# Making the gate's constants in two steps instead of one

## The chip, the cores and the metric

The kernel runs on one core of a Trainium2 chip. The metric is the device time of one execution in microseconds (us), as the median of several. Five engines work side by side, each through its own list of instructions in a fixed order: TensorE (PE; its weight loads are shown as PEld), VectorE (DVE), ScalarE (ACT), GpSimd (POOL) and SyncE (SP), whose queue issues the loads. An instruction that waits holds up everything behind it on its engine.

## The reference, cut to what matters

An attention stage feeds a mixture of experts (four experts, each token gets a weighted sum of all), and that feeds a second mixture in which each token goes to one of eight experts. The change concerns the numbers that choose this expert:

```python
logits = x @ w_gate + modality_bias[modality_id]   # x: 1152 x 512, w_gate: 512 x 8
e_idx = np.argmax(logits, axis=1)
probs = softmax(logits)
gate_w = probs[np.arange(N), e_idx]
# for every expert e, on the tokens with e_idx == e:
out[mask] = gate_w[mask, None] * (np.maximum(x[mask] @ w1[e], 0.0) @ w2[e])
```

## The kernel before

**Tiling.** Tokens are worked on in four chunks of 256, 256, 256 and 384 (numbered 0 to 3), the 1024 hidden units of an expert in eight slices f = 0 to 7. float32 operands are split into a high and a low part, and a product is made of three matmuls (high by high, high by low, low by high). For one slice and chunk, `mm1` (L695, 12 matmuls) makes the hidden values in PSUM, ACT writes their high part `hh` (L701), DVE their low part `hl` (L706), and `mm2` (L719 to L721, 3 matmuls for each 128 tokens) multiplies them by the second weight matrix. The third matmul of `mm2` is the first that needs `hl`. The weights are split the same way, by ACT (L404) and DVE (L674).

**Segments.** The first mixture runs as nine segments (an expert and some chunks each). The place of interest is segment 4: expert 3 on chunk 2, then on chunk 3. The text below calls its steps (2, f) and (3, f) by chunk and slice, so mm1(2, 3) is `mm1` of chunk 2, slice 3. In program order a step is mm1 of this slice, then mm2 of the slice before, and between them some extra work. By then the rows of chunks 0 and 1 are final, so their part of the second gate can start: 32 dot products on DVE (`dot`, L982: one block of 128 tokens by one column of `w_gate`; in the trace each is one SCALAR_TENSOR_TENSOR and one DVE_READ_ACCUMULATOR), one `dot` call after each step.

**The gate's constants.** `gate_consts` (L900 on) is called at step (2, 1). It has GpSimd make small tables; stores a table of empty slots, `ti`, to memory (`tab`, L935); loads the gate's weights as `wr` (L937), which DVE splits into `wg` (L939, L940); loads the same weights four more times, spread over all partitions, as `st` (L945), which GpSimd copies into rows `wgT` (L946), which the dots read; loads the modality numbers `mi` (L948) and the bias rows `mb` (L950); has DVE turn `mi` into floats `mf` (L952), PE transpose them (L954), and DVE make `bias` of the result (L957 to L964). `gate_cols` at step (2, 4) lets GpSimd copy the last two columns into `wgU` (L970), and the dots start behind it.

**What sets the order.** `ti`, `wr`, `mi` and a scratch tile of the bias share one buffer, named "tmp", and so each of them waits until the one before has been used up. Outside the parts with an order written by hand, the framework's scheduler places the instructions of each engine from their order in the program and their dependences; an instruction can land some steps before or after the place where the code has it.

Of the kernel before, what the change touches and what calls it, by code (L numbers as in the profile page):

```python
# [8 lines left out]
F32 = mybir.dt.float32  # L9
F32R = mybir.dt.float32r  # L10
# [3 lines left out]
ALU = mybir.AluOpType  # L14
# [14 lines left out]
KD = DM // 128  # L29
# [15 lines left out]
FIRST = {0: 0, 1: 0, 2: 4, 3: 4}  # L45
# [244 lines left out]
def moe_chain_kernel(ctx, tc, q, k, v, probs, w1, w2, mod, wg, mbias, v1, v2, out):  # L290
    nc = tc.nc
    N, E = probs.shape
    NT = N // 128
# [587 lines left out]
    m2p = {}  # L881
    G = {}
    R = {}
    V = v1.shape[0]
# [21 lines left out]
    def gate_consts():  # L906
        g = m2p["g"]

        def t(name, shape, dt=F32):
            G[name] = g.tile(shape, dt, tag=name, name=name, bufs=1)  # L910
            return G[name]

        def io(name, shape, pattern, base=0, cm=0):
            a = t(name, shape)
            nc.gpsimd.iota(a, pattern=pattern, base=base, channel_multiplier=cm, allow_small_or_imprecise_dtypes=True)

        io("e8", [128, V], [[-1, V]], base=V)
        io("ei", [128, V], [[1, V]])
        io("en", [128, V], [[SLOTS, V]])
        io("j128", [128, NBLK], [[128, NBLK]])  # L920
        io("thr", [128, NT], [[128, NT]])
        io("thr64", [128, NT], [[128, NT]], base=64)
        io("j", [128, NBLK], [[1, NBLK]])
        up = g.tile([128, 128], F32, tag="upf", name="upf", bufs=1)
        nc.gpsimd.memset(up, 1.0)
        nc.gpsimd.affine_select(out=up, in_=up, pattern=[[1, 128]], compare_op=ALU.is_gt, fill=0.0,
                                base=0, channel_multiplier=-1)
        nc.gpsimd.tensor_copy(out=t("up", [128, 128], BF16), in_=up)
        nc.gpsimd.memset(t("one", [128, 128], BF16), 1.0)
        G["tg"] = t("tg", [128, NT, 2])  # L930
        nc.gpsimd.iota(G["tg"][:, :, 0:1], pattern=[[128, NT]], base=0, channel_multiplier=1, allow_small_or_imprecise_dtypes=True)
        ti = g.tile([128, 256], F32, tag="tmp", name="ti", bufs=1)[:, 0:CAP // 64].rearrange("p (n c) -> p n c", c=2)
        nc.gpsimd.memset(ti, 0.0)
        nc.gpsimd.memset(ti[:, :, 0:1], float(N))
        nc.sync.dma_start(out=tab.rearrange("(p n) c -> p n c", p=128), in_=ti)  # L935
        wr = g.tile([128, 256], F32, tag="tmp", name="wr", bufs=1)[:, 0:KD * V].rearrange("p (k e) -> p k e", k=KD)
        nc.sync.dma_start(out=wr, in_=wg.rearrange("(k p) e -> p k e", p=128))  # L937
        w = t("wg", [128, KD, 2 * V], F32R)
        nc.vector.tensor_copy(out=w[:, :, 0:V], in_=wr)  # L939
        nc.vector.tensor_tensor(out=w[:, :, V:2 * V], in0=wr, in1=w[:, :, 0:V].bitcast(F32), op=ALU.subtract)  # L940

        t("wgT", [128, V - 2, DM])
        for qq in range(KD):
            st = G["st", qq] = m2p["raw"].tile([128, 128, V], F32, tag=f"r{qq + 3}", name=f"st{qq}")
            nc.sync.dma_start(out=st.rearrange("p d e -> p (d e)"), in_=wg[128 * qq:128 * qq + 128].rearrange("d e -> (d e)").partition_broadcast(128))  # L945
            nc.gpsimd.tensor_copy(out=G["wgT"][:, :, 128 * qq:128 * qq + 128], in_=st[:, :, 0:V - 2].rearrange("p d e -> p e d"))  # L946
        mi = g.tile([128, 256], F32, tag="tmp", name="mi", bufs=1)[0:NT].bitcast(I32).rearrange("p (n c) -> p n c", c=2)
        nc.sync.dma_start(out=mi, in_=mod.bitcast(I32).rearrange("(i p two) -> i p two", p=128, two=2))  # L948
        mb = g.tile([128, 2, V], F32, tag="mb", name="mb", bufs=1)
        nc.sync.dma_start(out=mb, in_=mbias.rearrange("m e -> (m e)").partition_broadcast(128))  # L950
        mf = g.tile([NT, 128], F32, tag="mf", name="mf", bufs=1)
        nc.vector.tensor_copy(out=mf, in_=mi[:, :, 0])  # L952
        pt = bank()
        nc.tensor.transpose(pt[:, 0:NT], mf, ident[:NT, :NT])  # L954
        m = g.tile([128, NT, 1], F32, tag="m", name="m", bufs=1)
        m0 = g.tile([128, NT, 1], F32, tag="m0", name="m0", bufs=1)
        nc.vector.tensor_copy(out=m, in_=pt[:, 0:NT])  # L957
        nc.vector.tensor_scalar(out=m0, in0=m, scalar1=-1.0, scalar2=1.0, op0=ALU.mult, op1=ALU.add)
        b = t("bias", [128, NT, V])
        b1 = g.tile([128, 256], F32, tag="tmp", name="b1", bufs=1)[:, 0:NT * V].rearrange("p (n e) -> p n e", n=NT)  # L960
        sh = [128, NT, V]
        nc.vector.tensor_tensor(out=b, in0=m0.to_broadcast(sh), in1=bc(mb[:, 0, :], sh, 1), op=ALU.mult)
        nc.vector.tensor_tensor(out=b1, in0=m.to_broadcast(sh), in1=bc(mb[:, 1, :], sh, 1), op=ALU.mult)
        nc.vector.tensor_tensor(out=b, in0=b, in1=b1, op=ALU.add)  # L964
# [695 lines left out]
    if True:  # L1660
# [87 lines left out]
        dots = [(i, x) for i in range(4) for x in range(V)]  # L1748
        for s, c, f in late:
            mm1(s, c, f)  # L1750
            if prev[0] in PAIR:
                s_mm2(*units[-1])
                ctxs.close()
                m2p["raw"] = ctx.enter_context(tc.tile_pool(name="m2raw", bufs=1, side="right", reuse_waits="tile"))
                m2p["g"] = ctx.enter_context(tc.tile_pool(name="gate", bufs=2, side="right", reuse_waits="tile"))
                y1 = m2p["g"].tile([128, 5, DM], F32, tag="y1", name="y1", bufs=1)
                yacc.extend(y1[:, t, :] for t in range(5))
            else:
                mm2(*prev)
            prev = (s, c, f)  # L1760
            if (s, c) == late[0][:2] and f < 4:
                w_split(1 + f % 2, s, 2 + f // 2)
                if f < 2:
                    w_load(1 + f, s, 3)
            r = runs.index((s, c))
            if c == SEG[s][1][0] and s > late[0][0] and f < 2:
                w_split(1 + f, s, 3)
                if len(SEG[s][1]) == 1:
                    w_load(1 + f, s + 1, 0)
            if f >= 6 and s == runs[r + 1][0] and c == SEG[s][1][-2]:  # L1770
                w_load(f - 5, s + 1, 0)
            if c == SEG[s][1][-1] and f >= 2:
                j = f // 2 - 1
                kind = 1 + f % 2
                w_split(kind, s + 1, j)
                w_load(kind, s + 1, j + 1)
            if (s, c, f) == (FIRST[2], 2, 1):
                gate_consts()
            if (s, c, f) == (FIRST[2], 2, 4):
                gate_cols()  # L1780
            if (s, c, f) > (FIRST[2], 2, 4) and dots:
                dot(*dots.pop(0))

        Q = build2()
# [42 lines left out]
```

## Time and profile before

| | us |
|---|---|
| median of 3 runs | 631.9 |
| lowest, highest | 631.59, 633.16 |
| profiled execution | 637.08 |
| its span | 635.1 |
| busy: PE / DVE / ACT / POOL | 602.2 / 423.3 / 277.3 / 83.9 |
| granted TensorE clock, mean | 0.977 of full speed |

The page cuts the span into 40 slices of 15.9 us each. PE is 90% busy or more in most of them; the low one in the middle is the slice around 260 us, where PE shows 4 tenths and its clock 7 tenths. A mean over the span hides such a place, so it is read by windows and by the timeline of each engine. In a timeline a row gives the start, the duration, the instruction, and in brackets how long its engine sat idle before it and what ended that wait.

### The profile page before, as it was taken

What the parts mean: (1) busy time and instruction counts of PE and PEld (TensorE: products, weight loads), DVE (VectorE), ACT (ScalarE), POOL (GpSimd) and SP (SyncE); (2) the same over time, 40 slices, a digit from 0 to 9 for tenths busy, and PEclk for the clock granted to TensorE, in tenths of its full rate; (3) what the DMA queues carried; (4) which work ended last, traced back from release to release, by engine and by line L of the source; (5) the groups of instructions that cost most, each with busy time, mean ns of one, the idle gap of its engine ahead of it and who ended that gap; (6) DMA issues with size and microseconds to landing.
All of it is one profiled execution on the core that took longest, in us unless ns stands there. A gap on an engine that the chain in (4) does not pass through costs nothing.

```text
span 635.1 us, 11351 instructions
## 1 busy us (share of the span) xinstructions
PE 602.2 (95%) x4229; PEld 527.7 (83%) x4234; DVE 423.3 (67%) x883; ACT 277.3 (44%) x628; POOL 83.9 (13%) x120
## 2 busy tenths in 40 slices
PE   7889999999999999499999999999999987999994
PEld 4678888889998888399999989989988876898883
DVE  4988777769759956697342355449765768658781
ACT  4955256544435443013311334213243543559581
POOL 3342123100000001600000000020130142101011
PEclk8989999999999999799999999999999997999998
DMA  7999944103423345401330346505496221868930
GB/s 148 158 220 217 225 126 130 35 2 99 133 67 100 101 132 160 146 1 51 118 99 1 100 133 199 166 33 101 102 343 188 82 68 42 279 195 255 309 134 20
DMA packets 91890, 82.87 MB, mean 130 GB/s; under 512 B 36391, under 2 KB 73648, under 8 KB 91826
## 3 DMA queue, kind: packets, MB, share of 16 engines
q1 hardware_dynamic: 89906, 77.33, 43.7%
q0 software_dynamic: 1920, 4.73, 2.2%
q8 instruction: 35, 0.57, 0.4%
q14 instruction: 29, 0.24, 0.1%
HBM read 81.69 MB, written 5.07 MB: 137 GB/s over the span
## 4 chain that ended last, share of the span: by engine, by line
PE 85%; DVE 4%; issue 4%; DMA 2%; ACT 1%; POOL 1%; another core or an unknown queue 1%; SPq 1%; POOLq 0%; ACTq 0%
PE ps L695 27%; PE ps L719 11%; PE ps L721 10%; PE ps L720 10%; PE ps L1432 7%; PE ps L809 5%; PE ps L1455 2%; PE ps L1454 2%; PE ps L1456 2%; PE ps L585 1%; DMA kraw<-in_k_dram 1%; PE ps L400 1%; DMA st<-in_moe_w_gate_dram 1%; PE ps L456 1%
## 5 line engine op out<-in xcount | busy, mean ns | idle before, releaser
L695 PE MATMUL ps<-xhi,w1h 128*128 128x256 f32 (+1 forms) x416 | 128.0, 308 | 0.0
L695 PE MATMUL ps<-xlo,w1h 128*128 128x256 f32 (+1 forms) x416 | 125.7, 302 | 0.3 <-DVE xlo L599 0.3
L695 PE MATMUL ps<-xhi,w1l 128*128 128x256 f32 (+1 forms) x416 | 125.6, 302 | 0.0
L701 ACT ACTIVATE hh<-ps 128x256 fp32r<-128x256 f32 (+1 forms) x104 | 43.0, 414 | 165.1 <-PE ps L695 153.3
L719 PE MATMUL ps<-w2h,hh 128*128 128x512 f32 x240 | 96.6, 403 | 0.0
L706 DVE SCALAR_TENSOR_TENSOR hl<-ps,hh 128x256 fp32r<-128x256 f32 (+1 forms) x104 | 47.8, 461 | 72.0 <-ACT hh L701 71.6
L721 PE MATMUL ps<-w2h,hl 128*128 128x512 f32 x240 | 94.8, 395 | 0.7 <-DVE hl L706 0.7
L720 PE MATMUL ps<-w2l,hh 128*128 128x512 f32 x240 | 94.4, 393 | 0.0
L695 PEld LDWEIGHTS ps<-xhi,w1h 128*128 128x128 f32 x416 | 79.7, 191 | 4.8 <-issue 0.6
L695 PEld LDWEIGHTS ps<-xlo,w1h 128*128 128x128 f32 x416 | 79.6, 191 | 4.4 <-DVE xlo L599 0.5
L695 PEld LDWEIGHTS ps<-xhi,w1l 128*128 128x128 f32 x416 | 79.5, 191 | 0.0
L674 DVE TENSOR_TENSOR w2l<-raw,w2h 128x1024 fp32r<-128x1024 f32 x36 | 45.5, 1264 | 31.2 <-ACT w2h L404 31.2
L404 ACT ACTIVATE w1h<-raw 128x1024 fp32r<-128x1024 f32 x46 | 48.6, 1056 | 17.8 <-PE ps L695 11.6
L404 ACT ACTIVATE w2h<-raw 128x1024 fp32r<-128x1024 f32 x33 | 35.0, 1061 | 47.0 <-PE ps L721 44.4
L721 PEld LDWEIGHTS ps<-w2h,hl 128*128 128x128 f32 x240 | 45.1, 188 | 11.9 <-DVE hl L706 1.2
L719 PEld LDWEIGHTS ps<-w2h,hh 128*128 128x128 f32 x240 | 45.1, 188 | 6.6 <-issue 0.4
L720 PEld LDWEIGHTS ps<-w2l,hh 128*128 128x128 f32 x240 | 45.2, 188 | 5.9
L1333 DVE TENSOR_TENSOR w2l<-r,w2h 128x1024 fp32r<-128x1024 f32 x28 | 33.9, 1220 | 14.5 <-ACT w2h L404 14.5
L674 DVE TENSOR_TENSOR w1l<-raw,w1h 128x1024 fp32r<-128x1024 f32 x30 | 36.6, 1220 | 7.9 <-ACT w1h L404 7.5
L404 ACT ACTIVATE w2h<-r 128x1024 fp32r<-128x1024 f32 x28 | 29.4, 1057 | 17.0 <-PE ps L1456 9.3
L1432 PE MATMUL ps<-xh,w1h 128*128 128x256 f32 x128 | 36.0, 281 | 0.0
L1432 PE MATMUL ps<-xl,w1h 128*128 128x256 f32 x128 | 35.8, 280 | 0.0
(328 smaller groups left out, 1179.7 us busy)
## 6 DMA issues: line engine op xcount, KB each, us to landing
raw<-in_moe_w_dram SPq DMA_DIRECT2D x85, 512.0 KB
r<-in_moe_w_dram SPq DMA_DIRECT2D x35, 512.0 KB
raw<-in_moe_w_dram SPq DMA_DIRECT2D x16, 256.0 KB
v<-in_v_dram SPq DMA_DIRECT2D x32, 80.0 KB
kraw<-in_k_dram SPq DMA_DIRECT2D x16, 147.0 KB
qraw<-in_q_dram SPq DMA_DIRECT2D x16, 147.0 KB
vq<-in_v_dram SPq DMA_DIRECT2D x8, 288.0 KB
ys<-y SPq DMA_DIRECT2D x9, 256.0 KB
```

The lines of the kernel that those rows point to most:

```text
L404: e.activation(out=out, in_=in_, func=ACTF.Copy, scale=scale)
L674: e.tensor_tensor(out=l, in0=W.pop(("raw", kind, s, j)), in1=h.bitcast(F32), op=ALU.subtract)
L695: nc.tensor.matmul(o, wt[:, kk, fs], xt[:, kk, :], start=(kk == 0 and m == 0), stop=(kk == KD - 1 and m == 2))
L701: nc.scalar.activation(out=hh, in_=o, func=ACTF.Relu)
L706: nc.vector.scalar_tensor_tensor(out=hl, in0=o, scalar=0.0, in1=hh.bitcast(F32), op0=ALU.max, op1=ALU.subtract)
L719: nc.tensor.matmul(a, hh, hi[:, g, :], start=(f == 0), stop=False)
L720: nc.tensor.matmul(a, hh, lo[:, g, :], start=False, stop=False)
L721: nc.tensor.matmul(a, hl, hi[:, g, :], start=False, stop=(f == NF - 1))
L809: nc.tensor.matmul(o, w[:, n, f], x[:, k], start=start and k == 0 and q == 0, stop=k == 1 and q == 2, skip_group_check=not start)
L1333: e.tensor_tensor(out=l, in0=R["raw", u], in1=h.bitcast(F32), op=ALU.subtract)
L1432: nc.tensor.matmul(pt, wt[:, kk, fs], xt[:, kk, :], start=(i == 0), stop=(i == 3 * KD - 1))
L1454: nc.tensor.matmul(o, hh[:, ts], hi[:, f % 2, :], start=(f == 0), stop=False)
```

## The change

`gate_consts` keeps GpSimd's work and all the loads. The split of `wr` into `wg`, the floats, the transpose and the bias go into a new step, `gate_bias`. It is called at step (3, 2), with `gate_cols` behind it, which moves there from (2, 4); the dots start after (3, 2) in the code. `wr` gets a buffer of its own, so only `ti`, `mi` and the scratch tile are left to share "tmp".

```diff
-        wr = g.tile([128, 256], F32, tag="tmp", name="wr", bufs=1)[:, 0:KD * V].rearrange("p (k e) -> p k e", k=KD)
+        wr = t("wr", [128, KD, V])
         nc.sync.dma_start(out=wr, in_=wg.rearrange("(k p) e -> p k e", p=128))
-        w = t("wg", [128, KD, 2 * V], F32R)
-        nc.vector.tensor_copy(out=w[:, :, 0:V], in_=wr)
-        nc.vector.tensor_tensor(out=w[:, :, V:2 * V], in0=wr, in1=w[:, :, 0:V].bitcast(F32), op=ALU.subtract)
...
         nc.sync.dma_start(out=mb, in_=mbias.rearrange("m e -> (m e)").partition_broadcast(128))
+        G["in"] = wr, mi, mb
+
+    def gate_bias():
+        g = m2p["g"]
+        wr, mi, mb = G["in"]
+        w = G["wg"] = g.tile([128, KD, 2 * V], F32R, tag="wg", name="wg", bufs=1)
+        nc.vector.tensor_copy(out=w[:, :, 0:V], in_=wr)
+        nc.vector.tensor_tensor(out=w[:, :, V:2 * V], in0=wr, in1=w[:, :, 0:V].bitcast(F32), op=ALU.subtract)
         mf = g.tile([NT, 128], F32, tag="mf", name="mf", bufs=1)
...
-        b = t("bias", [128, NT, V])
+        b = G["bias"] = g.tile([128, NT, V], F32, tag="bias", name="bias", bufs=1)
...
-            if (s, c, f) == (FIRST[2], 2, 4):
+            if (s, c, f) == (FIRST[2], 3, 2):
+                gate_bias()
                 gate_cols()
-            if (s, c, f) > (FIRST[2], 2, 4) and dots:
+            if (s, c, f) > (FIRST[2], 3, 2) and dots:
                 dot(*dots.pop(0))
```

Every instruction stays; what moves is where the scheduler puts them. PE before, from mm2(2, 0) on (`hl_3350` and `hl_3409` are the low parts of slices 0 and 1, `ps_3488` is the result of mm1(2, 2)):

```order
L721 MATMUL ps_3416<-w2h_3233,hl_3350 128x512
L719 MATMUL ps_3412<-w2h_3233,hh_3408 128x512
L720 MATMUL ps_3412<-w2l_3234,hh_3408 128x512
L721 MATMUL ps_3412<-w2h_3233,hl_3409 128x512
L719 MATMUL ps_3416<-w2h_3233,hh_3408 128x512
L720 MATMUL ps_3416<-w2l_3234,hh_3408 128x512
L721 MATMUL ps_3416<-w2h_3233,hl_3409 128x512
L954 MATMUL ps_3477<-ident_84,mf_3475 128x9
L695 MATMUL ps_3488<-xhi2_93,w1h_3324 128x256
L695 MATMUL ps_3488<-xlo2_97,w1h_3324 128x256
```

PE now at the same place (`ps_3472` is the result of mm1(2, 2)):

```order
L721 MATMUL ps_3416<-w2h_3233,hl_3350 128x512
L695 MATMUL ps_3472<-xhi2_93,w1h_3324 128x256
L695 MATMUL ps_3472<-xlo2_97,w1h_3324 128x256
L695 MATMUL ps_3472<-xhi2_93,w1l_3325 128x256
L695 MATMUL ps_3472<-xhi2_93,w1h_3324 128x256
L695 MATMUL ps_3472<-xlo2_97,w1h_3324 128x256
L695 MATMUL ps_3472<-xhi2_93,w1l_3325 128x256
L695 MATMUL ps_3472<-xhi2_93,w1h_3324 128x256
L695 MATMUL ps_3472<-xlo2_97,w1h_3324 128x256
L695 MATMUL ps_3472<-xhi2_93,w1l_3325 128x256
```

The transpose of `mf` no longer stands ahead of mm1(2, 2), and mm1(2, 2) now comes before mm2(2, 1). The transpose is now behind mm2(3, 1), ahead of mm1(3, 3):

```order
L719 MATMUL ps_3672<-w2h_3233,hh_3660 128x512
L720 MATMUL ps_3672<-w2l_3234,hh_3660 128x512
L721 MATMUL ps_3672<-w2h_3233,hl_3661 128x512
L959 MATMUL ps_3713<-ident_84,mf_3711 128x9
L695 MATMUL ps_3731<-xhi3_94,w1h_3324 128x384
L695 MATMUL ps_3731<-xlo3_98,w1h_3324 128x384
```

DVE before, from `hl` of slice 1 on (`hl_3502` would be that of slice 2):

```order
L706 SCALAR_TENSOR_TENSOR hl_3409<-ps_3395,hh_3408 128x256
L939 CAST wg_3455<-wr_3453 128x4x8
L940 TENSOR_TENSOR wg_3455<-wr_3453,wg_3455 128x4x8
L982 SCALAR_TENSOR_TENSOR junk_3566,l_3595<-y0_99,wgT_3458 128x512 x3
L952 CAST mf_3475<-mi_3471 9x128
L982 SCALAR_TENSOR_TENSOR junk_3566,l_3595<-y0_99,wgT_3458 128x512
L957 COPY m_3479<-ps_3477 128x9
L982 SCALAR_TENSOR_TENSOR junk_3566,l_3595<-y0_99,wgT_3458 128x512
L958 TENSOR_SCALAR m0_3480<-m_3479 128x9
L963 TENSOR_TENSOR b1_3484<-m_3479,mb_3473 128x72
L962 TENSOR_TENSOR bias_3483<-m0_3480,mb_3473 128x72
L982 SCALAR_TENSOR_TENSOR junk_3566,l_3595<-y0_99,wgT_3458 128x512
```

DVE now at the same place (`hl_3486`, `hl_3513` and `hl_3540` belong to slices 2, 3 and 4):

```order
L706 SCALAR_TENSOR_TENSOR hl_3409<-ps_3395,hh_3408 128x256
L954 CAST wg_3708<-wr_3453 128x4x8
L955 TENSOR_TENSOR wg_3708<-wr_3453,wg_3708 128x4x8
L706 SCALAR_TENSOR_TENSOR hl_3486<-ps_3472,hh_3485 128x256
L706 SCALAR_TENSOR_TENSOR hl_3513<-ps_3499,hh_3512 128x256
L957 CAST mf_3711<-mi_3468 9x128
L987 SCALAR_TENSOR_TENSOR junk_3725,l_3763<-y0_99,wgT_3455 128x512
L706 SCALAR_TENSOR_TENSOR hl_3540<-ps_3526,hh_3539 128x256
```

The `hl` of slices 2 and 3 now stand ahead of `mf` and of every dot; before, they stood behind eight of the dots. The short instructions of the bias have moved down into chunk 3. There DVE's list now reads, from the `hl` of step (3, 2) (`hl_3690`) to that of step (3, 3) (`hl_3745`):

```order
L706 SCALAR_TENSOR_TENSOR hl_3690<-ps_3676,hh_3689 128x384
L987 SCALAR_TENSOR_TENSOR junk_3725,l_3763<-y0_99,wgU_3724 128x512 x2
L962 COPY m_3715<-ps_3713 128x9
L987 SCALAR_TENSOR_TENSOR junk_3725,l_4490<-y0_99,wgT_3455 128x512
L963 TENSOR_SCALAR m0_3716<-m_3715 128x9
L968 TENSOR_TENSOR b1_3720<-m_3715,mb_3470 128x72
L967 TENSOR_TENSOR bias_3719<-m0_3716,mb_3470 128x72
L674 TENSOR_TENSOR w2l_3758<-raw_3620,w2h_3757 128x1024
L969 TENSOR_TENSOR bias_3719<-bias_3719,b1_3720 128x72
L987 SCALAR_TENSOR_TENSOR junk_3725,l_4490<-y0_99,wgT_3455 128x512
L674 TENSOR_TENSOR w1l_3792<-raw_3706,w1h_3791 128x1024
L706 SCALAR_TENSOR_TENSOR hl_3745<-ps_3731,hh_3744 128x384
```

Before, the two `hl` of these steps had only two splits of weights (L674) between them; now dots and the bias stand there too.

SP's queue before, around the gate's loads:

```order
L666 DMA raw_3646<-in_moe_w2_dram 128x2x512
L945 DMA st0_3459<-in_moe2_w_gate_dram 128x1024
L935 DMA tab_101<-ti_3449 128x164
L945 DMA st1_3462<-in_moe2_w_gate_dram 128x1024
L945 DMA st2_3465<-in_moe2_w_gate_dram 128x1024
L937 DMA wr_3453<-in_moe2_w_gate_dram 128x4x8
L945 DMA st3_3468<-in_moe2_w_gate_dram 128x1024
L950 DMA mb_3473<-in_moe2_modality_bias_dram 128x16
L664 DMA raw_3735<-in_moe_w1_dram 128x4x256
L948 DMA mi_3471<-in_moe2_modality_id_dram 9x256
```

SP's queue now:

```order
L666 DMA raw_3620<-in_moe_w2_dram 128x2x512
L937 DMA wr_3453<-in_moe2_w_gate_dram 128x4x8
L942 DMA st0_3456<-in_moe2_w_gate_dram 128x1024
L935 DMA tab_101<-ti_3449 128x164
L942 DMA st1_3459<-in_moe2_w_gate_dram 128x1024
L942 DMA st2_3462<-in_moe2_w_gate_dram 128x1024
L942 DMA st3_3465<-in_moe2_w_gate_dram 128x1024
L945 DMA mi_3468<-in_moe2_modality_id_dram 9x256
L947 DMA mb_3470<-in_moe2_modality_bias_dram 128x16
L664 DMA raw_3706<-in_moe_w1_dram 128x4x256
```

`wr` is now the first of the gate's loads, and `mi` comes ahead of `mb` and of the next load of weights.

## Rows read from the trace of the kernel before

**Rows 1.** Windows: busy us of PE, PEld, DVE, ACT, POOL; clock; DMA share, GB/s

```profile
259.72:267.47 7.75, 0.01 (x2) 0.01 (x1) 4.77 (x10) 0.00 (x0) 5.54 (x6) 0.60 0.37 123
267.47:272.32 4.85, 4.85 (x25) 4.83 (x26) 4.78 (x19) 0.38 (x1) 0.00 (x0) 0.58 0.00 0
255.75:272.32 16.57, 8.08 (x39) 6.83 (x38) 12.27 (x30) 0.77 (x2) 9.24 (x8) 0.69 0.40 124
```

**Rows 2.** Timeline of PE, from mm2(2, 0) to mm2(2, 3): start, duration

```profile
255.75 0.40 PE L719 MATMUL ps<-w2h,hh 128*128 128x512 f32 x1
...
258.52 0.50 PE L721 MATMUL ps<-w2h,hl 128*128 128x512 f32 x1 [0.74 <-DVE hl L706]
...
267.47 0.27 PE L954 MATMUL ps<-ident,mf 9*128 9x9 f32 x1 [7.75 <-DVE mf L952]
...
272.32 0.39 PE L719 MATMUL ps<-w2h,hh 128*128 128x512 f32 x1
...
273.72 0.28 PE L695 MATMUL ps<-xhi,w1h 128*128 128x256 f32 x1
...
275.15 0.39 PE L719 MATMUL ps<-w2h,hh 128*128 128x512 f32 x1
```

**Rows 3.** Timeline of DVE in the same stretch

```profile
258.05 0.41 DVE L706 SCALAR_TENSOR_TENSOR hl<-ps,hh 128x256 fp32r<-128x256 f32 x1
260.54 0.61 DVE L939 CAST wg<-wr 128x32 fp32r<-128x32 f32 x1 [2.07 <-DMA wr<-in_moe_w_gate_dram]
261.18 1.47 DVE L940 TENSOR_TENSOR wg<-wr,wg 128x32 fp32r<-128x32 f32 x1
264.71 1.09 DVE L982 SCALAR_TENSOR_TENSOR junk<-y,wgT 128x512 f32<-128x512 f32 x1 [2.06 <-POOL wgT L946]
...
265.85 0.69 DVE L982 SCALAR_TENSOR_TENSOR junk<-y,wgT 128x512 f32<-128x512 f32 x1
...
266.58 0.69 DVE L982 SCALAR_TENSOR_TENSOR junk<-y,wgT 128x512 f32<-128x512 f32 x1
...
271.18 0.42 DVE L706 SCALAR_TENSOR_TENSOR hl<-ps,hh 128x256 fp32r<-128x256 f32 x1
271.52 0.68 DVE L982 SCALAR_TENSOR_TENSOR junk<-y,wgT 128x512 f32<-128x512 f32 x1
```

**Rows 4.** Timeline of POOL in the same stretch

```profile
258.89 1.64 POOL L946 COPY wgT<-st 128x768 f32<-128x768 f32 x1 [0.26 <-DMA st<-in_moe_w_gate_dram]
...
261.05 1.55 POOL L946 COPY wgT<-st 128x768 f32<-128x768 f32 x1
...
263.12 1.55 POOL L946 COPY wgT<-st 128x768 f32<-128x768 f32 x1
264.62 0.64 POOL L970 COPY wgU<-st 128x256 f32<-128x256 f32 x1
```

**Rows 5.** Chain that ended last, one piece: start, us, what

```profile
254.28 4.56 DMA st<-in_moe_w_gate_dram
```

**Rows 6.** Timeline of SP: issues of the loads

```profile
250.25 0.46 SPq L945 DMA_DIRECT2D st<-in_moe_w_gate_dram  x1
...
255.49 0.38 SPq L937 DMA_DIRECT2D wr<-in_moe_w_gate_dram  x1
...
262.68 0.31 SPq L948 DMA_DIRECT2D mi<-in_moe_modality_id_dram  x1
```

**Rows 7.** Timeline of ACT, one `hh` of chunk 2

```profile
272.52 0.38 ACT L701 ACTIVATE hh<-ps 128x256 fp32r<-128x256 f32 x1 [1.51 <-PE ps L695]
```

**Rows 8.** Timeline of PE, steps of chunk 3

```profile
288.50 0.34 PE L695 MATMUL ps<-xhi,w1h 128*128 128x384 f32 x1
...
292.70 0.34 PE L695 MATMUL ps<-xhi,w1h 128*128 128x384 f32 x1
```

**Rows 9.** Timeline of DVE, steps of chunk 3

```profile
288.83 1.40 DVE L727 TENSOR_SCALAR y<-ps,p 128x512 f32<-128x512 f32 x2
...
292.70 1.22 DVE L674 TENSOR_TENSOR w1l<-raw,w1h 128x1024 fp32r<-128x1024 f32 x1
```

## The prediction

> **What bounds the kernel now.** PE is busy for 602.2 of the 635.1 us, so first the page's 40 slices: where is PE not full while the kernel is in mid-course? The slice around 260 us is the worst of the middle. Then the windows [rows 1]: in the 7.75 us from 259.72 to 267.47 PE did nothing, and in the 4.85 us behind that its granted clock was 0.58 of full speed, so most of it at the lower of the two levels (1.2 and 2.4 GHz). Then PE's timeline: it idled 0.74 us for an `hl`, and 7.75 us ahead of the transpose L954, for `mf` [rows 2]. Last, who was late ahead of `mf`. The order of DVE has `mf` behind the split of `wg` and three dots; the first dot started only at 264.71, when GpSimd's fourth copy into `wgT` was over [rows 3, 4]; these copies follow the loads of `st`, and the chain of waits holds such a load for 4.56 us from 254.28 [rows 5]. So PE waited for a transpose that nothing urgent needs, and through it for the gate's loads, copies and dots.
>
> **What this place costs.** From the start of mm2(2, 0) at 255.75 to that of mm2(2, 2) at 272.32 are 16.57 us. At full pace a mm2 of chunk 2 takes 1.40 (272.32 to 273.72) and a mm1 takes 1.43 (to 275.15) [rows 2]. The stretch holds two of each and the transpose, 0.27: 2 x 1.40 + 2 x 1.43 + 0.27 = 5.93. Lost: 16.57 - 5.93 = 10.64 us. Of this 8.49 is idle, and 1.7 is the clock: the two mm1 behind the wait took from 267.74 to 272.32, 4.58 instead of 2.86.
>
> **The change part by part.** *The transpose moves.* In the new order PE goes from mm2(2, 0) to mm1(2, 2), mm2(2, 1), mm1(2, 3) and so on, a step of 2.83 us, with no transpose in between. If nothing else is late, 10.64 us are gained. The transpose costs its 0.27 ahead of mm1(3, 3), where PE is full; that is already in the 5.93. Its `mf` is made some 20 us earlier (below), so it waits for nothing.
>
> *What is late next?* Every mm2(2, f) needs `hl` at its third matmul, 0.47 after its start. With PE never waiting these moments are 259.05 for slice 1, then every 2.83: 261.88, 264.71, 267.54, 270.37, 273.20 for slices 2 to 6. The next mm1, of chunk 3, is 0.68 longer, so 276.71 for slice 7; then steps of 4.20 [rows 8]: 280.2, 284.4, 288.6, 292.8 for (3, 0) to (3, 3).
>
> *`hl` of slices 1 to 3.* Slice 1 was done at 258.46 [rows 3]; the moment is 259.05, so even the old 0.74 us goes, since mm1(2, 2) now lies between. Ahead of slice 2 stand the two instructions on `wg`. `wr` was issued at 255.49 and took until 260.54 [rows 6, 3]; now it goes first, at 250.25, and with the same 5.05 us is there at 255.3. The two then cost between 0.3 us (an estimate, 0.15 each, under the 0.42 that DVE takes for 256 columns) and what they took before, 0.61 and 1.47. The second of them ended with a GpSimd copy that ran from 261.05 to 262.60 [rows 3, 4]: it was held. From 258.46 on the low end gives `hl` at about 259.7 (ACT needs 0.38 for `hh` behind mm1 [rows 7]); 0.61 + 1.47 + 0.41 gives 261.0. Both are ahead of 261.88, so this costs nothing. Slice 3 follows `hh` of mm1(2, 3), at about 262.4 against 264.71.
>
> *`mf` and the first dot.* `mi` waits for the store of `tab`, which had landed by 255.49, when `wr`, then behind it, was issued [rows 6]. Now `mi` goes at about 255.9, behind three `st`. The last `st` had landed when its copy began at 263.12 [rows 4], so I take 261 to 263.5 for `mi`. DVE reaches `mf` at 262.8 and must wait for GpSimd anyway: its four copies run as before, perhaps 0.25 later, since the first `st` is issued 0.38 later behind `wr`. First dot: 264.71 to 265.3, I take 264.95. It took 1.1 with GpSimd still copying [rows 3], and `hl` of slice 4 is done at 266.5 against 267.54.
>
> *The dots.* They are no longer spread over idle time; DVE now works from 264.95 without a pause. A dot costs 0.73 (265.85 to 266.58), an `hl` 0.34 (271.18 to 271.52) [rows 3], one of chunk 3 about 0.47 (an estimate from 0.34 and its 384 columns), a split of weights 1.14 (1.22 with its overlapped end), the two scalings 1.32 to 1.40 [rows 9]. Up to `hl` of (3, 1) the new order has one slow dot (1.10), 18 dots (13.14), four `hl` (1.36), one of chunk 3 (0.47), the scalings (1.32), a split (1.14) and that `hl` (0.55): 19.08, so 284.0 against 284.4. On the way slices 5, 6 and 7 have 0.7, 1.0 and 1.3 us to spare. From 283.95 to `hl` of (3, 3): seven dots (5.11), the `hl` of (3, 2) (0.47), two splits (2.28), the bias's five short instructions (an estimate, 0.5) and the `hl` (0.55): 8.91, so 292.9 against 292.8 plus the transpose's 0.27. This is the narrowest place: spare time 0.2. In the next step three dots and an `hl` stand, 2.7 us of 4.20, and the spare time grows. So DVE takes up nearly all the time that PE leaves it; I count 0.2 us for this place, bounds 0 and 0.6 (the first dot at 265.3 or a little later).
>
> *Loads.* The weights of the next segment go when DVE's splits free their buffers. By the sums above the first split of chunk 3 ends at 283.5, 10.4 us before the old 293.9 [rows 9], so with PE 0.2 later; the next two stand behind more dots than before, at most two each (1.5 us). A 512 KB load took 4.56 [rows 5], and the freed buffer serves a slice pair that is two steps (8.4) away. I count nothing.
>
> **Sum.** 10.64 - 0.2 = 10.4 us. Against the profiled execution's 637.08: 626.7. Behind this stretch the order of all engines is the old one and its loads follow PE's work, so the shift stays. The profiled execution is 5.2 above the median; I take the difference over unchanged: 631.9 - 10.4 = **621.5**.
>
> **The rivals.** *Part of it comes back on DVE.* Two places. If `wr` still landed only at 260.54 (behind the large loads) and the subtraction were held again to 262.65, `hl` of slice 2 would be done at 263.06, 1.2 us late: 622.7. The Trainium skill (SBUF — State Buffer, "Who interferes with whom") says that a DVE instruction with two SBUF inputs and a GpSimd instruction that reads SBUF shut each other out for a whole instruction; the held subtraction of the trace, 1.47 us, agrees. By that rule the price is 1.2; without it (0.15 for each of the two) `hl` would be done at 261.3 and nothing lost. If the first dot came 2 us later, at 267, the sums above would make PE wait 1.0 at slice 4 and about 1.9 in all by (3, 3): 623.4; both together 624.6. For it: at seven of the eight `hl` from slice 4 to (3, 3) DVE has no more than 1.4 us to spare. Against it: GpSimd's copies are the same, and the loads that they wait for are issued at the same time.
>
> *The wait comes back at another instruction, and grows.* `mf` now stands ahead of all dots and of `hl` of slice 4, and waits for `mi`. That `hl` must start by 267.1 and a dot goes ahead of it, so `mi` may land up to about 266. Each us beyond is a us of PE, and once PE stands long enough the 1.7 of clock comes on top. At 275 nothing would be left of the gain; beyond 277 the kernel is slower by over 0.3%, and at 280, 24 us after the issue, it takes 631.9 - 10.4 + 14 + 1.7 = 637.2. Against it: loads here took 4.6 to 5.1 [rows 5, 6].
>
> *The change does not do what it says.* Some other instruction holds PE at the old place and the loss stays: 631.9. Against it: the rows of PE's order have only mm1 and mm2 there, and each `hl` they need has its moment above.
>
> **How the numbers follow.** The forecast has 0.76. The first rival has 0.16 (622.5 to 625.0). The second has 0.05, of it 0.03 on the slower side, 0.01 within and 0.01 still faster. The third has 0.03. The range, 620.0 to 625.0, goes from the gain in full with 1.2 us for the spread of the runs to most of the first rival. A measurement of this kernel can tell about 0.3% (1.9 us) from no change: faster 0.76 + 0.16 + 0.01 = 0.93, within 0.01 + 0.03 = 0.04, slower 0.03.
>
> **What would show it.** In the new profile the windows around 260 us have PE full and its clock at 1.00 from 255 to 310; PE waits at no `hl` for over 0.5 us; the transpose stands in chunk 3 with no wait; DVE is full from 265 to 300 with the 32 dots. Wrong would be: an idle of PE ahead of an mm2's third matmul between 262 and 301 of over 1 us in sum, `mf` with an idle that ends on `mi`, or a stretch behind 310 that takes longer than before by more than 1 us.

## The result and the profile after

| | before | after |
|---|---|---|
| device time, median of 5 runs | 632.4 us (631.59 to 633.16) | 620.99 us (620.55 to 622.25) |
| the profiled execution, its span | 637.08, 635.1 | 620.99, 619.0 |
| mean granted clock of TensorE | 0.977 | 0.989 |
| mm2(2, 0) to mm2(3, 6), start to start | 60.10 | 50.14 |

The ratio of the times is 0.9825 (95% interval 0.9808 to 0.9842), so the kernel is 11.1 us faster (10.0 to 12.1). A second comparison, with nine runs of before and five of after, gave 620.91 against 631.1, ratio 0.9843 (0.9819 to 0.9867): 9.9 us (8.4 to 11.4). The prediction was 621.5, 10.4 us faster. The last line of the table is the best measure of the change itself: it goes from one matmul to the same matmul behind the whole disturbed stretch, in one execution. It will be called the **stretch** below. In before it runs from 255.75 [rows 2] to the start of mm2(3, 6):

```profile
315.85 0.39 PE L719 MATMUL ps<-w2h,hh 128*128 128x512 f32 x1
```

The windows of after, to be read against [rows 1]; the columns are busy us of PE, PEld, DVE, ACT and POOL, the granted clock, DMA's share and GB/s:

```profile
255.75:272.32 16.57, 16.48 (x104) 14.33 (x103) 11.22 (x22) 3.07 (x7) 9.86 (x8) 1.00 0.43 132
272.32:288.00 15.68, 15.68 (x83) 13.94 (x82) 15.19 (x42) 3.09 (x6) 0.00 (x0) 1.00 0.10 29
288.00:310.00 22.00, 22.00 (x115) 19.98 (x115) 17.20 (x43) 8.44 (x12) 0.00 (x0) 1.00 0.40 121
```

PE is busy for 16.48 of 16.57 us, where it was 8.08, and its clock is 1.00, where it was 0.69. DVE is busy for 15.19 of the next 15.68 us: it now does without a pause what it did in PE's idle time. PE's timeline, as in [rows 2]:

```profile
256.68 0.40 PE L719 MATMUL ps<-w2h,hh 128*128 128x512 f32 x1
...
267.97 0.39 PE L719 MATMUL ps<-w2h,hh 128*128 128x512 f32 x1
...
268.63 0.50 PE L721 MATMUL ps<-w2h,hl 128*128 128x512 f32 x1
...
271.10 0.39 PE L719 MATMUL ps<-w2h,hh 128*128 128x512 f32 x1
...
271.78 0.50 PE L721 MATMUL ps<-w2h,hl 128*128 128x512 f32 x1
...
274.24 0.39 PE L719 MATMUL ps<-w2h,hh 128*128 128x512 f32 x1
```

```profile
287.62 0.22 PE L959 MATMUL ps<-ident,mf 9*128 9x9 f32 x1
...
306.82 0.39 PE L719 MATMUL ps<-w2h,hh 128*128 128x512 f32 x1
```

From mm2(2, 0) at 256.68 to mm2(2, 4) at 267.97 are four steps of 2.82 us. In mm2(2, 4) and mm2(2, 5) the third matmul, which reads `hl`, starts 0.66 and 0.68 us after the first instead of 0.47; these steps are 3.13 and 3.14, so 0.3 us each are lost, 0.62 in sum (too short to be listed as waits). The transpose, now L959, stands in chunk 3 at 287.62 without an idle before it. DVE and POOL, against [rows 3, 4], and SP, against [rows 6]:

```profile
258.01 1.36 DVE L954 CAST wg<-wr 128x32 fp32r<-128x32 f32 x1
259.40 0.58 DVE L955 TENSOR_TENSOR wg<-wr,wg 128x32 fp32r<-128x32 f32 x1
260.12 0.42 DVE L706 SCALAR_TENSOR_TENSOR hl<-ps,hh 128x256 fp32r<-128x256 f32 x1
...
263.47 1.38 DVE L957 CAST mf<-mi 9x128 f32<-9x128 int32 x1
267.08 1.15 DVE L987 SCALAR_TENSOR_TENSOR junk<-y,wgT 128x512 f32<-128x512 f32 x1 [2.23 <-POOL wgT L943]
...
268.16 0.41 DVE L706 SCALAR_TENSOR_TENSOR hl<-ps,hh 128x256 fp32r<-128x256 f32 x1
...
271.31 0.42 DVE L706 SCALAR_TENSOR_TENSOR hl<-ps,hh 128x256 fp32r<-128x256 f32 x1
...
293.56 0.55 DVE L706 SCALAR_TENSOR_TENSOR hl<-ps,hh 128x384 fp32r<-128x384 f32 x1
```

```profile
256.98 2.34 POOL L943 COPY wgT<-st 128x768 f32<-128x768 f32 x1 [12.35 <-PE ps L695]
259.27 0.67 POOL L975 COPY wgU<-st 128x256 f32<-128x256 f32 x1
260.78 1.73 POOL L943 COPY wgT<-st 128x768 f32<-128x768 f32 x1 [0.84 <-DMA st<-in_moe_w_gate_dram]
...
265.35 1.70 POOL L943 COPY wgT<-st 128x768 f32<-128x768 f32 x1
```

```profile
251.16 0.46 SPq L937 DMA_DIRECT2D wr<-in_moe_w_gate_dram  x1
251.67 0.49 SPq L942 DMA_DIRECT2D st<-in_moe_w_gate_dram  x1
...
255.20 1.29 SPq L942 DMA_DIRECT2D st<-in_moe_w_gate_dram  x3
257.52 0.31 SPq L945 DMA_DIRECT2D mi<-in_moe_modality_id_dram  x1
```

The first dot starts at 267.08, again when GpSimd's fourth copy into `wgT` is over. As mm2(2, 0) starts 0.93 us later in this execution than in that of before (the stages ahead differ by that), the moment that answers to the trace of before is 266.15, not 264.71 [rows 3]. So `hl` of slices 4 and 5, at 268.16 and 271.31, come a little late.

### The profile page after: what moved, and what is told of

Same layout as the page of the kernel before. It is cut to its first block, busy times and chain, and to the rows that moved or that the text cites. A ratio compares the mean times of both kernels' runs of the same rounds, so it can differ in the third digit from the quotient of the medians.

```text
span 619.0 us, 11355 instructions
## 1 busy us (share of the span) xinstructions
PE 599.5 (97%) x4234; PEld 524.6 (85%) x4234; DVE 423.0 (68%) x883; ACT 277.3 (45%) x628; POOL 85.3 (14%) x120
## 5 line engine op out<-in xcount | busy, mean ns | idle before, releaser
L695 PE MATMUL ps<-xhi,w1h 128*128 128x256 f32 (+1 forms) x416 | 126.7, 305 | 0.0
L695 PEld LDWEIGHTS ps<-xhi,w1h 128*128 128x128 f32 x416 | 78.4, 188 | 4.9 <-issue 0.6
L695 PEld LDWEIGHTS ps<-xlo,w1h 128*128 128x128 f32 x416 | 78.3, 188 | 4.3 <-DVE xlo L599 0.4
L674 DVE TENSOR_TENSOR w2l<-raw,w2h 128x1024 fp32r<-128x1024 f32 x36 | 44.2, 1228 | 26.2 <-ACT w2h L404 26.2
L404 ACT ACTIVATE w1h<-raw 128x1024 fp32r<-128x1024 f32 x46 | 48.6, 1056 | 14.3 <-PE ps L695 11.4
L674 DVE TENSOR_TENSOR w1l<-raw,w1h 128x1024 fp32r<-128x1024 f32 x30 | 36.6, 1220 | 6.4 <-ACT w1h L404 6.1
```

The costliest lines, as they stand in the source:

```text
L404: e.activation(out=out, in_=in_, func=ACTF.Copy, scale=scale)
L674: e.tensor_tensor(out=l, in0=W.pop(("raw", kind, s, j)), in1=h.bitcast(F32), op=ALU.subtract)
L695: nc.tensor.matmul(o, wt[:, kk, fs], xt[:, kk, :], start=(kk == 0 and m == 0), stop=(kk == KD - 1 and m == 2))
```

## The experiments

The theory on trial, A: PE lost what it waited for a late `mf`, and for an `hl` that stood behind the late `mf` and the dots; what was late itself came from GpSimd's copies. The rivals: B, the own buffer of `wr` is the gain; C, the later start of the dots is; D, a transpose ahead of chunk 3 costs by its place, whoever is late. All runs in one table first. Each ratio is to the runs of before that were made beside it, whose medians lay between 631.1 and 633.08. "First dot" and "first copy" (of `st` into `wgT`) count from the start of mm2(2, 0). Full pace is what the best two traces show, 49.51. In e9 the order of DVE has the bias and `hl` of slice 4 ahead of the first dot, so its dot is late without harm.

| run | stretch, us | first copy | first dot | median, us | ratio to before |
|---|---|---|---|---|---|
| before (three profiles) | 60.10, 60.50, 60.43 | -0.41, -0.68, -0.39 | 8.96, 8.42, 8.73 | 632.4 | |
| after (two profiles) | 50.14, 50.92 | 0.30, 0.72 | 10.40, 11.21 | 620.99, 620.91 | 0.9825, 0.9843 |
| e1, only `wr`'s buffer | 59.81 | 0.33 | 10.40 | 632.88 | 1.0001 (0.9969 to 1.0032) |
| e2, bias at (2, 2) | 55.42 | 0.22 | 10.26 | 629.3 | 0.9948 (0.992 to 0.9977) |
| e3, bias at (2, 3) | 53.42 | 0.54 | 11.01 | 626.52 | 0.9891 (0.9857 to 0.9926) |
| e4, `wr` in tmp | 49.63 | -0.40 | 9.88 | 622.36 | 0.9846 (0.9806 to 0.9887) |
| e6, a copy on ACT | 49.51 | 0.62 | 8.91 | 619.77 | 0.9824 (0.9804 to 0.9843) |
| e7, both of these | 49.51 | -0.57 | 7.97 | 620.64 | 0.9838 (0.9817 to 0.9859) |
| e8, bias at (2, 4) | 50.02 | 0.45 | 10.55 | 621.34 | 0.9849 (0.9828 to 0.987) |
| e9, `mi` first | 50.47 | 0.18 | 10.96 | 622.33 | 0.983 (0.9792 to 0.9868) |

**e1: before, with `wr`'s own buffer alone.**

```diff
-        wr = g.tile([128, 256], F32, tag="tmp", name="wr", bufs=1)[:, 0:KD * V].rearrange("p (k e) -> p k e", k=KD)
+        wr = t("wr", [128, KD, V])
```

> The kernel before with one part of the change alone: wr has a buffer of its own. The transpose still stands ahead of mm1(2, 2); on DVE mf now comes right behind the two instructions on wg, ahead of all dots, but hl of slice 2 is behind five dots. Theory A (PE loses what it waits at the transpose for mf, and then at hl behind the dots): in the changed kernel's time scale PE is at the transpose at 258.1, mf is done between 261.4 and 264.9 and PE waits 3 to 7 us there; the first dot cannot start before the fourth GpSimd copy is over, 267.1, so hl of slice 2 is done at about 272 and not at 262.8, where a PE at full pace wants it: 9.3 us lost in all, against 621.0 - 0.6 at full pace: 629.7 (629 to 631). Theory B (the own buffer of wr, and its earlier load, is the gain): about 621.

Measured: no gain, 1.0001. B falls. The loss has only another face; first the list of PE's waits (us in total, times, longest), then two windows, behind the first wait and around the second, and DVE:

```profile
PE ps L954 <- DVE mf L952: 3.8, 1, 3.8
...
PE ps L721 <- DVE hl L706: 2.3, 1, 2.3
```

```profile
263.90:269.15 5.25, 5.25 (x25) 5.25 (x25) 1.82 (x6) 0.39 (x1) 4.00 (x4) 0.50 0.05 18
271.40:276.05 4.65, 4.00 (x16) 3.65 (x17) 4.25 (x14) 0.00 (x0) 0.00 (x0) 0.63 0.01 4
```

```profile
262.98 0.65 DVE L952 CAST mf<-mi 9x128 f32<-9x128 int32 x1 [2.74 <-DMA mi<-in_moe_modality_id_dram]
267.33 1.12 DVE L982 SCALAR_TENSOR_TENSOR junk<-y,wgT 128x512 f32<-128x512 f32 x1 [3.70 <-POOL wgT L946]
...
271.58 0.42 DVE L706 SCALAR_TENSOR_TENSOR hl<-ps,hh 128x256 fp32r<-128x256 f32 x1
```

`mf` waits for `mi` until 262.98 and PE for `mf`, 3.80 us instead of 7.75; then PE waits 2.27 us for the `hl` of slice 2, which stands behind five dots, and the dots start at 267.33. That is theory A, but its price was too low: the stretch lost 10.3 us, not 9.3. What I had left out is the clock behind the second wait. This `hl` was done at 272.00, as expected, which made PE's third matmul 8.7 us late (272.05 for 263.33, an estimate from the terms of the prediction's sum); the 16 matmuls behind it then took 4.00 us where full pace is 2.36, another 1.6. Behind the first wait the clock was down too: the two mm1 there took 5.25 us at a granted clock of 0.50 (2.86 at full pace). But this cost nothing more, since PE then had to wait for the `hl` anyway.

**e2 and e3: after, with `gate_bias` one or two slices later than e1, at (2, 2) and (2, 3).** The diff is e2's; e3 has (2, 3) in it.

```diff
-            if (s, c, f) == (FIRST[2], 3, 2):
+            if (s, c, f) == (FIRST[2], 2, 2):
                 gate_bias()
+            if (s, c, f) == (FIRST[2], 3, 2):
                 gate_cols()
```

> The changed kernel with gate_bias called at (2, 2) instead of (3, 2); gate_cols and the dots stay at (3, 2). The transpose stands ahead of mm1(2, 3), and hl of slice 3 is behind mf, three dots and the bias. Theory A: PE is at the transpose at 260.9, mf is ready at about 264.9, then hl of slice 3 comes at about 270.4 where a PE at full pace wants it at 265.6: 4 us of wait at the transpose or in sum 4.8 us: 624.3 to 626, I take 625.2. Theory B (own buffer of wr): 621. Theory C (the dots' later start is the gain, wherever the transpose is): 621.

> The changed kernel with gate_bias called at (2, 3). The transpose stands ahead of mm1(2, 4), at 263.7; DVE's order up to mf is that of the changed kernel, and hl of slice 4 is behind three dots and the bias instead of one dot. Theory A: PE waits 1.2 us at the transpose, and hl of slice 4 comes 2.1 us behind the moment at which a PE at full pace wants it: 620.4 + 2.1 = 622.5 (622 to 623.5). Theories B and C: 621.

Measured: 3.3 and 6.9 us faster than before, where after has 10 to 11; the stretches 55.42 and 53.42 fall between those of e1 and after. C falls: the dots are called as late as in after, and much of the loss is there. Both stretches are longer than I expected (5.9 and 3.9 us over full pace, for 4.8 and 2.1), again mostly because the clock was left out: in each the 16 matmuls behind the wait for `hl` took 3.9 and 3.7 us where full pace is 2.36. The waits of PE, in e2 (two lines) and in e3 (one line), then a window of e3 behind its wait, and e3's DVE:

```profile
PE ps L721 <- DVE hl L706: 3.6, 2, 3.3
...
PE ps L959 <- DVE mf L957: 0.8, 1, 0.8
```

```profile
PE ps L721 <- DVE hl L706: 2.3, 2, 2.1
```

```profile
271.90:275.69 3.79, 3.74 (x17) 3.52 (x18) 3.62 (x11) 0.00 (x0) 0.00 (x0) 0.62 0.00 0
```

```profile
264.20 0.54 DVE L957 CAST mf<-mi 9x128 f32<-9x128 int32 x1
268.56 1.14 DVE L987 SCALAR_TENSOR_TENSOR junk<-y,wgT 128x512 f32<-128x512 f32 x1 [3.82 <-POOL wgT L943]
...
271.47 0.42 DVE L706 SCALAR_TENSOR_TENSOR hl<-ps,hh 128x256 fp32r<-128x256 f32 x1
```

In e3 the transpose waits for nothing: `mf` was ready. PE waits 2.14 us for the `hl` of slice 4 at 271.47, behind the dots that began at 268.56, and then runs at 0.62 of full clock. So the place of `gate_bias` works in two ways: through the transpose on PE, and through the order on DVE, since the scheduler puts the bias and the dots ahead of an `hl` that it takes to be later. These two runs can't part the one from the other; e8 and e9 do.

**e4: after, with `wr` back in the shared buffer.**

```diff
-        wr = t("wr", [128, KD, V])
+        wr = g.tile([128, 256], F32, tag="tmp", name="wr", bufs=1)[:, 0:KD * V].rearrange("p (k e) -> p k e", k=KD)
```

> The changed kernel with wr back in the shared buffer tmp: its load goes behind the store of tab, the split of wg comes behind hl of slice 3, mi waits for that split, mf comes behind three dots; the transpose stays in chunk 3. Theory A: mf late costs nothing, since its transpose is needed only at 289: 620.4 to 621.6, as the changed kernel. Theory B (the own buffer is the gain): 629 to 632.

Measured: as fast as after within what the runs can tell, 0.9846 against 0.9825 and 0.9843, and its stretch is shorter, 49.63. The median, 622.36, lies 0.8 above the range that I had expected, on a chip where before took 633.08. So the own buffer is not needed, which B demands. Two lines of DVE show why:

```profile
264.63 1.17 DVE L987 SCALAR_TENSOR_TENSOR junk<-y,wgT 128x512 f32<-128x512 f32 x1 [1.61 <-POOL wgT L943]
...
267.40 0.21 DVE L957 CAST mf<-mi 9x128 f32<-9x128 int32 x1
```

The first dot starts 9.88 us behind mm2(2, 0), for 10.40 in after, and `mf` is made only at 267.40, behind three dots, and nobody waits for it.

**e5: after once more.**

> The changed kernel once more, beside the next three on one chip. From the start of mm2(2, 0) to that of mm2(3, 6) it took 50.1 us in its first profile (before: 60.1), of which 0.6 are two late hl, of slices 4 and 5, behind a first dot that waits for GpSimd's fourth copy into wgT. Expected: 50.1 again, 621 in all; the start of the stretch and the wait for w2l near 510 us may differ by some us from execution to execution, as they did between the profiles so far.

Measured: 620.91, as expected, but the stretch took 50.92. GpSimd's second copy, DVE and PE:

```profile
260.48 1.73 POOL L943 COPY wgT<-st 128x768 f32<-128x768 f32 x1 [1.65 <-DMA st<-in_moe_w_gate_dram]
```

```profile
266.77 1.14 DVE L987 SCALAR_TENSOR_TENSOR junk<-y,wgT 128x512 f32<-128x512 f32 x1 [3.87 <-POOL wgT L943]
...
267.84 0.41 DVE L706 SCALAR_TENSOR_TENSOR hl<-ps,hh 128x256 fp32r<-128x256 f32 x1
```

```profile
268.31 0.50 PE L721 MATMUL ps<-w2h,hl 128*128 128x512 f32 x1 [0.83 <-DVE hl L706]
```

The second `st` held the copies 1.65 us, the first dot came 11.21 us behind mm2(2, 0), and PE waited 0.83 us for `hl` of slice 4 (1.09 of its step) and 0.3 for that of slice 5. So the remaining loss follows the first dot: 9.88 (e4) gave 0.12, 10.40 gave 0.62, 11.21 gave 1.41. After these 0.83 us of idle the clock stayed at 1.00.

**e6 and e7: the fourth copy into `wgT` on ScalarE; e7 with `wr` in tmp besides.**

```diff
-            nc.gpsimd.tensor_copy(out=G["wgT"][:, :, 128 * qq:128 * qq + 128], in_=st[:, :, 0:V - 2].rearrange("p d e -> p e d"))
+            copy(nc.scalar if qq == KD - 1 else nc.gpsimd, G["wgT"][:, :, 128 * qq:128 * qq + 128], st[:, :, 0:V - 2].rearrange("p d e -> p e d"))
```

> The changed kernel with the fourth copy into wgT on ScalarE, which is idle for 2.4 us between two hh there; GpSimd keeps three. If the late hl of slices 4 and 5 come from the first dot's wait for GpSimd's fourth copy, the first dot starts some 1.7 to 2.3 us earlier, both hl are in time and the stretch takes 49.5 instead of 50.1: 620.4. If they come from DVE having too much to do in itself (32 dots without a pause), the loss of 0.6 stays: 621.0. If the copy on ScalarE takes more than 2.4 us, hh of slice 5 is late by the rest: 621 to 623.

> Both: the fourth copy into wgT on ScalarE, and wr back in the shared buffer tmp, with which the stretch took 49.6 us. If the two late hl are all that is left in this stretch, it takes 49.5 and no less, 620.4 in all, as with one of the two edits. If GpSimd's earlier start gives more than these 0.6 us, it is below 49.3.

Measured: both stretches 49.51. ACT's copy and the first dot of e6:

```profile
262.28 1.80 ACT L404 ACTIVATE wgT<-st 128x768 f32<-128x768 f32 x1 [0.79 <-DMA st<-in_moe_w_gate_dram]
263.95 0.41 ACT L701 ACTIVATE hh<-ps 128x256 fp32r<-128x256 f32 x1
```

```profile
264.18 0.78 DVE L987 SCALAR_TENSOR_TENSOR junk<-y,wgT 128x512 f32<-128x512 f32 x1 [2.02 <-ACT wgT L404]
...
264.90 0.41 DVE L706 SCALAR_TENSOR_TENSOR hl<-ps,hh 128x256 fp32r<-128x256 f32 x1
```

The copy fits between two `hh`, the first dot comes 8.91 us behind mm2(2, 0), and `hl` of slice 4 is in time. So the two late `hl` come from GpSimd's copies and not from DVE's load, and behind them nothing is left to gain in this stretch: e7's dot is another 0.9 us earlier and its stretch the same. e6's median is 619.77 against 620.91 for after on the same chip. That this kernel is faster than after is not shown by the times, whose intervals overlap; what is shown is a stretch that is shorter by 0.6 to 1.4 us.

**e8: after, with `gate_bias` at (2, 4).** The diff is that of e2 with (2, 4).

> The changed kernel with gate_bias called at (2, 4) instead of (3, 2): the transpose stands one step of 2.8 us later than in the run at (2, 3), and hl of slice 4 is again behind one dot only. Theory A (a late mf, and the hl that stand behind the dots, are what PE loses): nothing is late but the two hl by 0.3 us each, so 621 and 50.1 us for the stretch; the runs at (2, 2) and (2, 3) had 55.4 and 53.4. If a transpose and its bias in chunk 2 cost by themselves, whatever DVE's order: above 51 us and 622.

Measured: 621.34 and 50.02, as A has it. The transpose stands in chunk 2, one slice behind e3's, waits for nothing, and `hl` of slice 4 has one dot ahead of it. So a transpose in chunk 2 costs no more by its place than one in chunk 3, and D falls.

**e9: before, with `mi` loaded first and `mf` made at once.** One step at (2, 1), `wr` in tmp and dots from (2, 4) on, as before.

```diff
+        mi = g.tile([128, DM], F32, tag="prod", name="mi", bufs=1)[0:NT, 0:256].bitcast(I32).rearrange("p (n c) -> p n c", c=2)
+        nc.sync.dma_start(out=mi, in_=mod.bitcast(I32).rearrange("(i p two) -> i p two", p=128, two=2))
+        mf = g.tile([NT, 128], F32, tag="mf", name="mf", bufs=1)
+        nc.vector.tensor_copy(out=mf, in_=mi[:, :, 0])
         io("e8", [128, V], [[-1, V]], base=V)
...
-        mi = g.tile([128, 256], F32, tag="tmp", name="mi", bufs=1)[0:NT].bitcast(I32).rearrange("p (n c) -> p n c", c=2)
-        nc.sync.dma_start(out=mi, in_=mod.bitcast(I32).rearrange("(i p two) -> i p two", p=128, two=2))
...
-        mf = g.tile([NT, 128], F32, tag="mf", name="mf", bufs=1)
-        nc.vector.tensor_copy(out=mf, in_=mi[:, :, 0])
```

> The kernel before with its gate in one step at (2, 1), wr in tmp and the dots from (2, 4) on, all as they were; only mi is loaded first, into a buffer that is free then, and mf is made at once. The transpose stands even earlier, inside mm2(2, 1), and DVE has mf right behind hl of slice 1, the bias ahead of all dots and hl of slice 4 ahead of the first dot. Theory A (what PE lost was a late mf, and hl behind it and behind dots, and not the transpose's place as such): the transpose waits between 0.1 us and 1.2 us (if the cast of mf is held by GpSimd's copy, as it was for 1.38 us in the changed kernel), no hl is late, the stretch takes 49.5 to 50.7 us, 620.4 to 621.6 in all. If the gain needs the transpose out of chunk 2: 629 to 632.

Measured: 622.33, ratio 0.983, stretch 50.47, as A has it for the stretch; the median is 0.7 above the range expected, on a chip where before took 632.93. The gain is there with nothing moved out of chunk 2, and the transpose even earlier than in before. PE, DVE and POOL at that place:

```profile
257.76 0.23 PE L954 MATMUL ps<-ident,mf 9*128 9x9 f32 x1 [0.90 <-DVE mf L920]
```

```profile
256.41 1.29 DVE L920 CAST mf<-mi 9x128 f32<-9x128 int32 x1
```

```profile
255.26 2.36 POOL L950 COPY wgT<-st 128x768 f32<-128x768 f32 x1 [12.23 <-PE ps L695]
```

PE waits 0.90 us for `mf`, whose cast ran from 256.41 to 257.70 beside a GpSimd copy from 255.26 to 257.62; no `hl` is late. This is theory A without the change: make `mf` early, with no `hl` behind it and the dots, and the transpose is harmless in chunk 2.

**e10 and e11: before, two more profiles.**

> The kernel before once more, for its profile: the stretch takes 60.1 us again; the wait of PE for w2l near 520 us, 5.1 us in the first profile, was 0.7 in the kernel with wr's own buffer and absent in four others. If it belongs to the kernel before, it is 5 us again; if it differs from execution to execution, it is anything between 0 and 5.

> The same for a third profile: if the wait for w2l goes with the kernel before, again about 5 us; if not, another value than in the run ahead of it.

The wait of PE for `w2l` in the last stage, in the first profile of before (PE, then ACT), in e10 and in e11:

```profile
527.52 0.79 PE L1455 MATMUL ps<-w2l,dh 128*128 128x512 f32 x1 [5.11 <-DVE w2l L1333]
```

```profile
525.44 0.38 ACT L1437 ACTIVATE dh<-ps 128x256 fp32r<-128x256 f32 x1 [5.20 <-remote]
```

```profile
524.93 0.50 PE L1455 MATMUL ps<-w2l,dh 128*128 128x512 f32 x1 [2.18 <-issue]
```

```profile
523.65 0.50 PE L1455 MATMUL ps<-w2l,dh 128*128 128x512 f32 x1 [0.66 <-DVE w2l L1333]
```

5.11, 2.18 and 0.66 us (the 2.18 listed as issue, a wait for nothing that the profile shows): it differs from execution to execution. e4 had it with 3.81, e3 with 2.37, e9 with 0.89 and, some steps later, 2.26 for `w1l`, e1 and e2 with 0.7; after had it in neither profile, and e6, e7 and e8 had none. So it does not need the order of before (e4), but of the six profiles with `gate_bias` at (2, 4) or (3, 2) only that one has it, and of the seven others all; whether the order bears on it is not shown. The profile says only that ACT waited 5.20 us for something remote, that is, for no instruction of this core that it shows; what that is stays open.

## Why the prediction came out right, step by step

- **10.64 us are lost at this place.** Right. The undisturbed stretch of e6 and e7 is 49.51 against 60.10: 10.59. All of it came back in those, 9.96 and 9.18 in the two profiles of after.
- **The transpose waits for nothing in chunk 3; `hl` of slices 1 to 3 are in time.** Right. The two instructions on `wg` took 1.36 and 0.58 us, 1.94 in sum against bounds of 0.3 and 2.08, and nobody waited for them.
- **`mi` lands between 261 and 263.5, `mf` costs nothing.** Right. `mf` started at 263.47, 262.5 in the time of before, so `mi` was there by then; where DVE can be seen to wait for the load, in e1, it was issued at 257.34 and held DVE until 262.98, 5.6 us. The cast took 1.38 us, which I had not counted; it lay in DVE's wait for the first dot.
- **The first dot at 264.95 (264.71 to 265.3).** Wrong, and the step that failed: "its four copies run as before, perhaps 0.25 later". Brought to the time of before it was 266.15 in the one profile and 266.96 in the other. Of the 1.44 us in the first profile 0.96 stand at the start of the second copy, which came 4.10 behind mm2(2, 0) for 3.14 in before, after 0.84 of waiting for its `st`. The other 0.49 came behind it: from there to the end of the fourth copy GpSimd took 6.27 us for 5.78, as a copy took 1.70 to 1.73 for 1.55 to 1.64. That second `st` was issued as early as before, 1.48 us ahead of mm2(2, 0), but its copy started 5.58 us behind the issue, for 4.61 in before (254.28 to 258.89). In the seven profiles that load `wr` first this took 5.57 to 6.40 us, in the five with the old order of loads 4.05 to 5.09. Whether it is `wr` ahead of them or the third `st` that now follows at once was not tried apart; e9, with a small load ahead but two `st` at once, has 4.97. The first copy too starts later in the six kernels that load `wr` first, 0.22 to 0.72 us behind mm2(2, 0), for 0.68 ahead of it to 0.18 behind in the other six profiles.
- **0.2 us lost, at `hl` of (3, 3).** Wrong place and too little. Nothing was lost at (3, 3): that `hl` started at 293.56, and PE's step there has its usual 4.21. From the first dot to the end of that `hl` DVE took 27.0 us where I had counted 27.9, so it made up most of the late start. The loss was at slices 4 and 5, 0.62 us in the first profile and 1.41 in the second, where I had counted 1.0 and 0.7 us to spare. This is the second place of my first rival: a first dot 2 us late was to cost 1.0 at slice 4 and 1.9 in all. In e5 it was 2.0 late (266.96 for 264.95) and cost 1.09 at slice 4 and 1.4 in all: the rival's price holds at slice 4 and is too high by 0.5 in all. e5 also showed what I had named as signs of being wrong: its wait of 0.83 us is over 0.5, and its third matmuls of slices 4 and 5 started 1.2 us late in sum, for a bound of 1 (PE idle was 0.90 of it). So after shows the forecast's gain less a part of this rival's price, and how large a part differs between executions. As the sum took 0.2 for all of it, 10.4 was 0.4 to 1.2 too much for the stretch.
- **The held subtraction of the first rival.** `wr` was early, so the rival's condition did not come about; but the subtraction was held again, by a shorter copy: it took 0.58 us and ended at 259.98, 0.04 behind GpSimd's copy into `wgU` (259.27 to 259.94). It is so in all 13 profiles, for the subtraction (0.58 to 1.61 us) and for the cast of `wg` (0.18 to 1.37): each ended 0.03 to 0.06 us behind a copy. So no run shows the 0.15 that I took for either alone, and the 0.61 of before was a held time too. The cast of `mf` shows both cases. It has 9x128 elements and took 0.21 us in the five profiles where no copy ran beside it (the three of before, e4, e7), and 0.30 to 1.38 in the eight others, and in each of these it ended 0.07 to 0.09 us behind the copy that was running. The section of the Trainium skill that the prediction names (SBUF — State Buffer, "Who interferes with whom") also says that a cast can enter a mode of DVE that takes both ports and then shuts GpSimd out or is shut out. The traces agree, as far as casts that are shut out go.
- **The second rival, a late `mi`.** Did not come. Of the kernels with this order of DVE the nearest is e8, where `mf` was 0.37 us late on `mi` at 264.16, and nothing followed from it.
- **The third, the loss stays with another instruction.** Not in after, but it is just what e1 shows: the transpose's wait halved, and the rest came back at `hl` and in the clock behind it.
- **Nothing changes behind the stretch, and the difference can be taken over to the median.** Right in kind: no new wait stands there. The profiled execution of before was 5.2 above the median of the first three runs. It held the wait for `w2l`, 5.11 us, and matmuls at a granted clock of 0.50 in the 3.4 us behind; a wait of this size can't have stood in most runs (e11, with 0.66, took 631.5). That is why the profiled executions differ by 16.1 us and the runs, by their ratio, by 11.1. From mm2(3, 6) to the end before took 319.3, 316.0 and 312.7 us in its three profiles, after 312.2 and 312.4, e4 318.8. So what of the 11.1 goes beyond the stretch's 9.96 can't be put down to the change, and can't be ruled out as part of it: this wait and the start of mm2(2, 0), between 254.75 and 257.55 in these traces, differ by more between executions. That the median came out 0.5 from the forecast is in part luck: the stretch gave less than the sum, and the runs differed by more than the stretch.

## What to carry over

Ask of a wait of TensorE not only what it waits for but whether that operand could have been ready: here a small transpose did little or no harm where its input was made early (e9, 0.90 us) or where it stood late enough for its input to be there (e8, after). What follows from it must not stand ahead of an operand that is needed sooner (e3), and moving one buffer alone only moved the wait (e1). When a wait is taken away, look for the work that lay in its shadow, here 32 dots on DVE, and check when its first one can start; what is left of the loss follows that start (e5, e6). Give the idle time its second price too, the clock of the matmuls behind it.

## What the hardware showed that was not expected

- A DVE cast of 9x128, with a single input, took 0.21 us with no GpSimd copy beside it and up to 1.38 with one: in all eight such profiles it ended 0.07 to 0.09 us behind that copy. Such short instructions ahead of an `hl` are worth a look at what GpSimd does then.
- GpSimd's copies of 128x768 took 1.55 or 1.56 us where PE stood still (before, e10, e11, e1), 1.62 where PE ran at a granted clock of 0.50 (e1), 1.64 where it ran for half of the copy, and 1.66 to 1.74 where it ran at 1.00 for most of it; copies beside a DVE split of weights are left out. In before a DMA share of 0.86 or of 0.04 beside them made no difference. The cause was not tried, and spans on GpSimd are rough; 0.49 us of the late first dot goes with it.
- After waits of 2.14 us (e3) and 2.27 us (e1) of PE the 16 matmuls behind took 3.7 and 4.0 us instead of 2.36, at a granted clock of about 0.6; after 0.83 and 0.90 us (e5, e9) it stayed at 1.00.
- The same load of 512 KB (the second `st`) had its copy start 4.61 us behind its issue in before, 5.09 in e4, 5.58 and 6.40 in the two profiles of after.
- In the last stage PE's wait for `w2l` was 0.66 to 5.11 us in three executions of one kernel, the longest behind a wait of ACT on something remote; its cause is open.
